# Attention loads in a routed network: even and odd partitions in place of partition blocks

## The chip, the cores and the metric

The kernel runs on one core of one Trainium2 chip. The metric is the device time of one execution in microseconds, the median of several executions; less is better. The kernel uses five engines: TensorE (PE in the rows), VectorE (DVE), ScalarE (ACT), GpSimd (POOL) and SyncE (SP), and 16 DMA engines that move data between the chip's main memory and SBUF, the on-chip memory of 128 partitions. SP issues nearly all the transfers that this text is about.

## The reference, cut to what matters

An attention over windows comes first, then two mixtures of experts on its result. Only the attention is touched by the change.

```
B, H, S, D = 4, 8, 768, 64
for c in range(24):                       # chunks of 32 queries
    k_full = concat([mem_k, k[l_start:r_end]])     # 8 memory rows + up to 56 of context
    v_full = concat([mem_v, v[l_start:r_end]])
    scores = 0.125 * q_c @ k_full.T       # per batch and head
    a = softmax(scores)
    out[c] = a @ v_full
x = out as 3072 tokens x 512
x = moe(x, w_gate, w1, w2)                # 8 experts, capacity 384 tokens each
return moe2(x, ...)                       # top 2 of 8 experts, noisy gate
```

## The kernel before, in words

**Units and tiles.** The attention works on 24 tiles of 128 tokens with all 8 heads. Two tiles make a unit, so there are 12 units. Each unit has three buffers in SBUF, and there are three sets of them (`NB`, line 238): `q` (128 partitions, 4 head pairs, 256 queries), `k` (128 partitions, 2 halves, 4 head pairs, 312 keys) and `v` (128 partitions, 2 halves, 4 head pairs, 8 chunks, 65 columns). Two heads form a pair, and one matmul serves both: 64 of the 128 partitions hold the first head of the pair, the other 64 the second. So that the heads don't mix, `k` and `v` have two halves along the free dimension. Half 0 holds data in the first head's 64 partitions and zeros in the rest; half 1 holds data in the second head's 64 partitions and zeros elsewhere. The zeros are written once, at the start (`clear`, line 259), and every load overwrites only the data.

**Which partitions.** In the kernel before, the first head sits in partitions 32 to 95 and the second in 0 to 31 and 96 to 127 (`lanes`, line 1972, orders the arrays in main memory in the same way). Half 0 of `k` or `v` is therefore one transfer of 64 neighbouring partitions, and half 1 is two transfers of 32 neighbouring partitions each.

**Loading.** `load(u)` (line 285) brings a unit in four groups, in this order: q, all of k, half 0 of v, half 1 of v. `paced` (line 275) sends them: before each group it issues a transfer of one element to a small tile called `behind` (line 278) that reads what the third group before has written, so SP stops there until that group has landed. At most three groups are on their way at a time. Line 280 issues the group's own transfers. All of this is one queue: what SP stops at holds everything behind it.

**Stages.** For each tile there are `scores` (line 296, q times k), `softmax` (line 310: VectorE's maximum and difference, then ScalarE's exponentials, in two instructions since the second head's keys stand in two pieces), `ptrans` (line 329, transposes on TensorE), `av` (line 338, times v), `norm`, `split`, `xtrans` and `logits`. `STAGES` (line 224) fixes the order in which the tiles' stages are issued, written out by hand, and each engine works in that order. After every second tile a further unit is loaded into the buffers that have come free. From tile 18 on, the results are stored to main memory with the same `paced`, behind the last loads. Then the routing of the first mixture of experts starts on VectorE and TensorE, and after it the experts' matrix products, in an order set by a planner with costs of its own (class `Pipe`), which the change does not touch.

Of the kernel before, what the change touches and what calls it, by code (L numbers as in the profile page):

```python
# [8 lines left out]
F32 = mybir.dt.float32  # L9
# [3 lines left out]
AF = mybir.ActivationFunctionType  # L13
# [222 lines left out]
def attention(ctx):  # L236
    nc, tc, t = ctx.nc, ctx.tc, ctx.t
    NB = 3
    KU = 4 * KP + LEFT + RIGHT
    with (  # L240
# [4 lines left out]
        bufs = []  # L245
        for i in range(NB):
            q = ld.tile([128, HP, 256], F32, name=f"q{i}")
            k = ld.tile([128, 2, HP, KU], F32, name=f"k{i}")
            v = ld.tile([128, 2, HP, 8, D + 1], F32, name=f"v{i}")
# [6 lines left out]
        xb = psT.tile([128, 2, 512], F32, name="xb")  # L256
        st = [dict() for _ in range(G)]

        def clear(i, j):
            x = bufs[i][j]  # L260
            if i:
                (nc.vector if i == 1 else nc.gpsimd).memset(x, 0.0)
                return
            for n, (p, h2) in enumerate(((0, 0), (32, 1), (96, 0), (64, 1))):
                (nc.gpsimd if j == 2 or n % 2 else nc.vector).memset(x[p : p + 32, h2], 0.0)

        def warm(n):
            some = ctx.ones16[:, :16].unsqueeze(1).to_broadcast([128, G - 1, 16])
# [6 lines left out]
        def paced(*dmas):  # L275
            if len(flown) >= AHEAD:
                n = len(flown) % 8
                nc.sync.dma_start(behind[:, n : n + 1], flown[-AHEAD])  # L278
            for out, src in dmas:
                nc.sync.dma_start(out, src)  # L280
            while len(out.shape) > 2:
                out = out[:, 0]
            flown.append(out[:1, :1])

        def load(u):
            q, k, v = bufs[u % NB]

            def part(x, src, a, b, h2):
                return x[a:b, h2], src[u, a:b]

            paced((q, t.qT[u]))
            paced(*[part(k, t.kT, *r) for r in ((32, 96, 0), (0, 32, 1), (96, 128, 1))])
            paced(part(v, t.vctx, 32, 96, 0))
            paced(*[part(v, t.vctx, *r) for r in ((0, 32, 1), (96, 128, 1))])

        def scores(i):
            q, k, v = bufs[(i // 2) % NB]
# [12 lines left out]
        def softmax(i):  # L310
            sv = st[i].pop("S").rearrange("p h a k -> p (h a) k")
            if (i * 128) % S == 0:
                nc.vector.memset(sv[:CH, :, :LEFT], NEG)
            if (i * 128 + 128) % S == 0:
                nc.vector.memset(sv[96:, :, KEYS - RIGHT :], NEG)
            mx = wk.tile([128, H], F32, tag="mx", name=f"mx{i}")
            p = wk.tile([128, H, KEYS], F32, tag="p", name=f"p{i}")
            nc.vector.tensor_reduce(mx, sv, axis=AX.X, op=ALU.max)
            nc.vector.tensor_tensor(p, sv, mx.unsqueeze(2).to_broadcast([128, H, KEYS]), op=ALU.subtract)
            pe = wk.tile([128, HP, 2 * KEYS], F32, tag="pe", name=f"pe{i}")  # L320
            ps = p.rearrange("p (h a) k -> p h a k", a=2)
            nc.scalar.activation(pe[:, :, 32:96], ps[:, :, 0], AF.Exp, scale=0.125)
            nc.scalar.activation(
                pe.rearrange("p h (b k) -> p h b k", b=4)[:, :, 0::3], ps[:, :, 1].rearrange("p h (b k) -> p h b k", b=2),
                AF.Exp, scale=0.125,
            )
            st[i]["pe"] = pe

# [141 lines left out]
                counts.pop()()  # L470

        later, counts = [], []
        load(0)
        ctx.early(ld)
        nc.scalar.preload_act_table_set("natural_log_exp_and_others")
        for i in range(NB):
            clear(i, 1)
            clear(i, 2)
            if i:
                load(i)  # L480
        stage = locals()
        for i in range(-2, G - 1):
            if i == 0:
# [8 lines left out]
            u = (i - 1) // 2 + NB  # L492
# [474 lines left out]
def constants():  # L967

    f, g = {}, {}
    f["e8f"] = np.tile(np.arange(E, 0, -1, dtype=np.float32), (128, 1))  # L970
    keep = np.ones((128, E, G), np.float32)
    keep[:, :, 0] = 0.0
    f["keep"] = keep
    f["keys"] = np.tile(np.array([2.0**20] + list(range(E - 1, 0, -1)), np.float32), (128, 1))
    f["cap2"] = np.tile(np.array([C2 - XN] + [C2] * (E - 1), np.float32), (128, 1))
    k0 = (np.arange(1, NT + 1, dtype=np.int64) - (NT + 1) // 2) << 28
    f["cand0"] = np.tile(np.where(k0 >= 0, k0, k0 ^ 0x7FFFFFFF).astype(np.int32).view(np.float32), (128, 1))
    for plan in (FAST, THRIFTY):
        jtab = [np.arange(1, n + 1) << sh for n, sh in zip(plan.nj[1:], plan.shifts[1:])] + [np.zeros(1)]
        f["jtab" + plan.name] = np.tile(np.concatenate(jtab).astype(np.int32), (128, 1))  # L980

    k0 = (np.arange(1, NH + 1, dtype=np.int64) - 64) << 25
    g["candh"] = np.tile(np.where(k0 >= 0, k0, k0 ^ 0x7FFFFFFF).astype(np.int32).view(np.float32), (128, 1))
    g["tri"] = np.triu(np.ones((128, 128), np.float32), 1)
    g["iota"] = np.tile(np.arange(128, dtype=np.float32), (128, 1))

    tok = np.arange(G)[None, :] * 128.0 + np.arange(128)[:, None] - NTOK // 2
    g["tokid"] = tok[:, :, None].astype(np.float32)
    g["slotid"] = (tok + (tok >= 0))[:, :, None].astype(np.float32)
    for low in (32, 128):  # L990
        g[f"cols{low}"] = np.tile(np.arange(128 // low * 3 if low < 128 else NA2, dtype=np.float32) - FAR / low, (128, 1))
    return f, g
# [970 lines left out]
def host_layout(i):  # L1963
    q, k, v, mk, mv = i["q"], i["k"], i["v"], i["mem_k"], i["mem_v"]
    NC = S // CH
    f = {}

    U = B * S // 256
    KU = 4 * KP + LEFT + RIGHT
    qT = q.reshape(B, HP, 2, S // 256, 256, D).transpose(0, 3, 2, 5, 1, 4)  # L1970

    lanes = np.r_[64:96, 0:64, 96:128]
    f["qT"] = qT.reshape(U, 128, HP, 256)[:, lanes]


    kb = np.zeros((B, H, NC // 2 * KP + LEFT + RIGHT, D), np.float32)
    vb = np.ones((B, H, NC // 2 * KP + LEFT + RIGHT, D + 1), np.float32)
    for src, mem, dst in ((k, mk, kb), (v, mv, vb)):
        src = np.pad(src, ((0, 0), (0, 0), (LEFT, RIGHT), (0, 0)))
        for m in range(NC // 2):  # L1980
            dst[:, :, KP * m : KP * m + WIN, :D] = src[:, :, 64 * m : 64 * m + WIN]
            dst[:, :, KP * m + WIN : KP * m + WIN + NMEM, :D] = mem
            dst[:, :, KP * m + WIN + NMEM : KP * m + KP, :D] = src[:, :, 64 * m + WIN : 64 * m + 64]
        dst[:, :, KP * (NC // 2) :, :D] = src[:, :, S:]
    kT = kb.reshape(B, HP, 2, -1, D).transpose(0, 2, 4, 1, 3)
    kT = np.stack([kT[..., 4 * KP * m : 4 * KP * m + KU] for m in range(S // 256)], axis=1)
    f["kT"] = kT.reshape(U, 128, HP, KU)[:, lanes]
    k0 = [KP * (c // 2) + CH * (c % 2) for c in range(NC)]
    vc = np.stack([vb[:, :, o : o + KEYS] for o in k0], axis=3)
    vc = vc.reshape(B, HP, 2, KEYS, S // 256, 8, D + 1).transpose(0, 4, 2, 3, 1, 5, 6)  # L1990
    f["vctx"] = vc.reshape(U, 128, HP, 8, D + 1)[:, lanes]
    f["noise"] = np.ascontiguousarray(i["moe2_noise"].reshape(G, 128, E).transpose(1, 0, 2))
    wg2 = np.concatenate([i["moe2_w_gate"], i["moe2_w_noise"]], axis=1)
    f["wg2"] = np.ascontiguousarray(wg2.reshape(KT, 128, 2 * E).transpose(1, 0, 2))
    for n, m in (("w1", "moe_w1"), ("x1", "moe2_w1")):
        f[n] = np.ascontiguousarray(i[m].reshape(E, KT, 128, 4, FF // 4).transpose(0, 3, 2, 1, 4)).reshape(E, 4, 128, 1024)
    for n, m in (("w2", "moe_w2"), ("x2", "moe2_w2")):
        f[n] = np.ascontiguousarray(i[m].reshape(E, 4, 2, 128, DM).transpose(0, 1, 3, 2, 4)).reshape(E, 4, 128, 1024)
    f["wg"] = np.ascontiguousarray(i["moe_w_gate"].reshape(KT, 128, E).transpose(1, 0, 2))
    f["id32"] = np.eye(128, dtype=np.float32)  # L2000
    for n, c in zip(("consts", "passing"), constants()):
        f[n] = np.concatenate([a.reshape(128, -1).view(np.float32) for a in c.values()], axis=1)
    return f
# [19 lines left out]
```

## Time and profile before

| | |
|---|---|
| median of 3 executions | 1055.89 us (1055.35 to 1056.14) |
| the profiled execution | 1053.0 us, of which the span from first to last instruction is 1051.2 us |
| TensorE busy in the span | 986.2 us (94%) |
| VectorE / ScalarE / GpSimd busy | 642.3 / 461.8 / 296.0 us |
| mean granted TensorE clock | 0.976 |

The span falls in three parts: the attention, up to about 130 us; the first routing, about 131 to 153 us; and the two mixtures of experts, up to the end. How to read the rows further down: times are microseconds from the start of the span; an arrow points from what is read to what is written (`k<-kT_dram` loads k from main memory); L280 is line 280; `SPq` is SP issuing a transfer, and its time is that of the issue, not of the transfer. A "DMA share" of 1.00 means that all 16 DMA engines had a packet in hand throughout.

### The profile page before, as it was taken

How to read it: one execution, taken by the hardware profiler on the slowest of the kernel's cores; microseconds unless marked ns; L12 is line 12 of the kernel's file. 1: busy time of each engine (PE TensorE's matmuls, PEld its weight loads, DVE VectorE, ACT ScalarE, POOL GpSimd, SP SyncE). 2: the span in 40 equal slices, each digit the busy share in tenths (PEclk: the TensorE clock that was granted, in tenths of full speed). 3: DMA queues.
4: the chain of work that ended last, by engine and by line, in shares of the span. 5: the costliest groups of instructions: out<-in, count | busy, mean ns of one | idle time of the engine just before them, and what ended most of it. 6: DMA issues, size and time to landing. Idle time of an engine off the chain costs nothing.

```text
span 1051.2 us, 21987 instructions
## 1 busy us (share of the span) xinstructions
PE 986.2 (94%) x8312; PEld 592.7 (56%) x8312; DVE 642.3 (61%) x2096; ACT 461.8 (44%) x817; POOL 296.0 (28%) x471
## 2 busy tenths in 40 slices
PE   7787649999999999998989999999999999999997
PEld 4676546767676676544555454455555555555553
DVE  6687775666666758695774846545455454564221
ACT  2576514444534446986506535245153351533110
POOL 6565414101102023101021323333233331232321
PEclk9899859999999999999999999999999999999999
DMA  8898833557578486959349748539367393664520
GB/s 238 255 267 235 304 137 123 186 159 210 169 225 203 151 203 192 305 165 201 62 105 268 241 133 244 140 106 260 95 203 176 88 286 87 167 116 110 115 66 31
DMA packets 147253, 184.61 MB, mean 176 GB/s; under 512 B 105558, under 2 KB 106070, under 8 KB 145608
## 3 DMA queue, kind: packets, MB, share of 16 engines
q1 hardware_dynamic: 129814, 131.74, 46.2%
q0 software_dynamic: 13872, 45.15, 14.7%
q10 hardware_dynamic: 3458, 6.30, 1.7%
q8 instruction: 66, 1.08, 0.5%
q14 instruction: 43, 0.35, 0.1%
HBM read 127.10 MB, written 32.44 MB: 152 GB/s over the span
## 4 chain that ended last, share of the span: by engine, by line
PE 71%; DMA 11%; DVE 6%; issue 5%; ACT 3%; SPq 2%; POOL 1%; ACTq 0%; POOLq 0%; DVEq 0%
PE m L68 55%; PE m2f L68 10%; DMA v<-vctx_dram 4%; PE rps L68 3%; DMA k<-kT_dram 1%; DMA yT<-rb 1%; SPq L280 1%; DMA xg<-xr,idx 1%; ACT junk L68 1%; SPq L278 1%; DMA xr<-rb 1%; PE slps L68 1%; PE sb L304 1%; DVE sloh L68 1%; DMA st<-x_dram 1%
## 5 line engine op out<-in xcount | busy, mean ns | idle before, releaser
L68 PEld LDWEIGHTS <-hT 128*128 128x128 f16 (+2 forms) x1800 | 143.5, 99 | 159.5 <-issue 5.1
L68 ACT ACTIVATE hT<-m 128x384 f16<-128x384 f32 (+2 forms) x152 | 75.6, 499 | 274.6 <-PE m L68 271.6
L68 DVE SCALAR_TENSOR_TENSOR hT<-m,hT 128x384 f16<-128x384 f32 (+2 forms) x152 | 86.4, 569 | 96.3 <-ACT hT L68 96.2
L68 ACT ACTIVATE junk<-st 128x1024 f16<-128x1024 f32 x108 | 113.6, 1052 | 61.4 <-DMA st<-x_dram 26.0
L68 PE MATMUL m2f<-st,hT 128*128 128x256 f32 x480 | 127.6, 398 | 0.6 <-ACT hT L68 0.6
L68 POOL DMA_INDIRECT out_dram<-pv,ts x47 | 48.9, 1040 | 257.5 <-DVE pv L68 99.3
L68 DVE SCALAR_TENSOR_TENSOR pv<-m,ys,pv 128x512 f32<-128x512 f32 (+2 forms) x47 | 33.5, 714 | 118.8 <-PE m L68 118.7
L68 PE MATMUL m<-xT,w_0h 128*128 128x384 f16 (+2 forms) x384 | 96.6, 331 | 2.8 <-DMA xT<-xg 2.8
L68 PE MATMUL m<-xT,w_2h 128*128 128x384 f16 (+2 forms) x384 | 96.7, 331 | 1.7 <-DVE hT L68 1.7
L68 PE MATMUL m<-xT,w_1h 128*128 128x384 f16 (+2 forms) x384 | 96.5, 331 | 0.0
L68 PE MATMUL m<-xT,w_3h 128*128 128x384 f16 (+2 forms) x384 | 96.4, 331 | 0.0
L68 PEld LDWEIGHTS m2f<-st,hT 128*128 128x128 f32 x480 | 83.4, 190 | 10.2 <-ACT hT L68 1.0
L68 PE MATMUL m<-w_3h,hT 128*128 128x512 f16 (+2 forms) x300 | 71.6, 345 | 1.4 <-DVE hT L68 1.4
L68 PE MATMUL m<-w_0h,hT 128*128 128x512 f16 (+2 forms) x300 | 72.7, 348 | 0.0
L68 PE MATMUL m<-w_1h,hT 128*128 128x512 f16 (+2 forms) x300 | 72.1, 347 | 0.0
L68 PE MATMUL m<-w_2h,hT 128*128 128x512 f16 (+2 forms) x300 | 71.5, 345 | 0.0
L68 PE MATMUL m<-xT,w_2l 128*128 128x384 f16 (+2 forms) x192 | 63.6, 331 | 0.0
L68 PE MATMUL m<-xT,w_1l 128*128 128x384 f16 (+2 forms) x192 | 63.6, 331 | 0.0
L68 PE MATMUL m<-xT,w_3l 128*128 128x384 f16 (+2 forms) x192 | 63.6, 331 | 0.0
L68 PE MATMUL m<-xT,w_0l 128*128 128x384 f16 (+2 forms) x192 | 63.6, 331 | 0.0
L68 POOL DMA_INDIRECT xg<-x,rows x54 | 53.2, 985 | 29.9 <-issue 11.7
L68 POOL DMA_INDIRECT xg<-xr,idx x24 | 25.0, 1040 | 129.1 <-DVE idx L68 39.0
(336 smaller groups left out, 1870.2 us busy)
## 6 DMA issues: line engine op xcount, KB each, us to landing
st<-w_dram SPq DMA_DIRECT2D x64, 512.0 KB
st<-x_dram SPq DMA_DIRECT2D x64, 512.0 KB
xr<-rb SPq DMA_DIRECT2D x24, 264.0 KB
x<-rb SPq DMA_DIRECT2D x24, 264.0 KB
v<-vctx_dram SPq DMA_DIRECT2D x12, 520.0 KB
v<-vctx_dram SPq DMA_DIRECT2D x24, 260.0 KB
q<-qT_dram SPq DMA_DIRECT2D x12, 512.0 KB
out_dram<-zero ACTq DMA_DIRECT2D x24, 256.0 KB
```

The costliest lines, as they stand in the source:

```text
L68: return f(*args, **kw)
L278: nc.sync.dma_start(behind[:, n : n + 1], flown[-AHEAD])
L280: nc.sync.dma_start(out, src)
L304: nc.tensor.matmul(sc[CH * c : CH * c + CH, hp], q[:, hp, CH * o : CH * o + CH], k[:, :, hp, k0 : k0 + KEYS], start=True, stop=True,)
```

## The change

The first head of a pair takes the even partitions and the second the odd ones (`lanes` becomes 0, 64, 1, 65, ...). Each half of `k` and of `v` is then one transfer of 64 partitions at every second partition. The exponentials of both heads are one instruction, which writes every second column. The buffers are cleared whole, half by half, by VectorE, ScalarE and GpSimd, all of it issued ahead of the first load, and the four small arrays of `ctx.early` are loaded after unit 0's q and k instead of after its v.

```
-        def clear(i, j):
-            x = bufs[i][j]
-            if i:
-                (nc.vector if i == 1 else nc.gpsimd).memset(x, 0.0)
-                return
-            for n, (p, h2) in enumerate(((0, 0), (32, 1), (96, 0), (64, 1))):
-                (nc.gpsimd if j == 2 or n % 2 else nc.vector).memset(x[p : p + 32, h2], 0.0)
+        def clear(i, j, *engines):
+            x = bufs[i][j].rearrange("p a h k -> p a (h k)" if j == 1 else "p a h c d -> p a (h c d)")
+            for h2, e in enumerate(engines):
+                if e is nc.scalar:
+                    e.activation(x[:, h2], zero.to_broadcast([128, x.shape[2]]), AF.Copy)
+                else:
+                    e.memset(x[:, h2], 0.0)
...
-            def part(x, src, a, b, h2):
-                return x[a:b, h2], src[u, a:b]
+            def part(x, src, h2):
+                return x[h2::2, h2], src[u, h2::2]
 
             paced((q, t.qT[u]))
-            paced(*[part(k, t.kT, *r) for r in ((32, 96, 0), (0, 32, 1), (96, 128, 1))])
-            paced(part(v, t.vctx, 32, 96, 0))
-            paced(*[part(v, t.vctx, *r) for r in ((0, 32, 1), (96, 128, 1))])
+            paced(*[part(k, t.kT, h2) for h2 in range(2)])
+            if not u:
+                ctx.early(ld)
+            for h2 in range(2):
+                paced(part(v, t.vctx, h2))
...
-            ps = p.rearrange("p (h a) k -> p h a k", a=2)
-            nc.scalar.activation(pe[:, :, 32:96], ps[:, :, 0], AF.Exp, scale=0.125)
             nc.scalar.activation(
-                pe.rearrange("p h (b k) -> p h b k", b=4)[:, :, 0::3], ps[:, :, 1].rearrange("p h (b k) -> p h b k", b=2),
-                AF.Exp, scale=0.125,
+                pe.rearrange("p h (k a) -> p h a k", a=2), p.rearrange("p (h a) k -> p h a k", a=2), AF.Exp, scale=0.125
             )
...
-        load(0)
-        ctx.early(ld)
+        zero = ld.tile([128, 1], F32, name="zero")
+        nc.vector.memset(zero, 0.0)
         nc.scalar.preload_act_table_set("natural_log_exp_and_others")
+        V_, S_, G_ = nc.vector, nc.scalar, nc.gpsimd
+        for i, (ke, ve) in enumerate((((V_, G_), (S_, V_)), ((G_, G_), (V_, S_)), ((S_, S_), (G_, V_)))):
+            clear(i, 1, *ke)
+            clear(i, 2, *ve)
         for i in range(NB):
-            clear(i, 1)
-            clear(i, 2)
-            if i:
-                load(i)
+            load(i)
...
-    lanes = np.r_[64:96, 0:64, 96:128]
+    lanes = np.arange(128).reshape(2, 64).T.ravel()
```

On SP, at the start of the program, the difference reads as follows (the minus is before, the plus is after; `k_106`, `v_107` and `q_105` are unit 0's buffers, `id`, `c_wg` and `c_noise` the small arrays of `ctx.early`).

```order
 L280 DMA q_105<-qT_dram 128x1024
-L280 DMA k_106<-kT_dram 64x1248
-L280 DMA k_106<-kT_dram 32x1248 x2
+L280 DMA k_106<-kT_dram 64x1248 x2
+L1911 DMA id_138<-id_dram 128x128
+L1888 DMA c_wg<-wg_dram 128x32
+L1888 DMA c_wg_142<-wg_dram 128x64
+L1888 DMA c_noise<-noise_dram 128x192
 L280 DMA v_107<-vctx_dram 64x2080
 L278 DMA behind<-q_105 1x1
-L280 DMA v_107<-vctx_dram 32x2080 x2
+L280 DMA v_107<-vctx_dram 64x2080
```

Two transfers of 32 partitions have become one of 64, in k and in v, and the four small arrays have moved up past both transfers of v.

On SP, in the middle of the loads, where one unit follows another (`k_109`, `v_110` and `q_108` belong to one unit, `q_111` to the next):

```order
 L278 DMA behind<-v_107 1x1
-L280 DMA k_109<-kT_dram 64x1248
-L280 DMA k_109<-kT_dram 32x1248 x2
+L280 DMA k_109<-kT_dram 64x1248 x2
 L278 DMA behind<-v_107 1x1
 L280 DMA v_110<-vctx_dram 64x2080
 L278 DMA behind<-q_108 1x1
-L280 DMA v_110<-vctx_dram 32x2080 x2
+L280 DMA v_110<-vctx_dram 64x2080
 L278 DMA behind<-k_109 1x1
 L280 DMA q_111<-qT_dram 128x1024
```

The order of the groups and of the waits (`behind`) is as before; a unit has five transfers of its own in place of seven.

On ScalarE, at the start (`pe` is the tile of exponentials, `p` the differences, `zero` a single column):

```order
-L475 ACT_TABLE_LOAD
-L322 ACTIVATE pe_208<-p_205 128x4x64
-L323 ACTIVATE pe_208<-p_205 128x4x2x32
+L474 ACT_TABLE_LOAD
+L263 ACTIVATE v_107<-zero 128x2080
+L263 ACTIVATE v_110<-zero 128x2080
+L263 ACTIVATE k_112<-zero 128x1248 x2
+L323 ACTIVATE pe_204<-p_201 128x4x2x64
```

Four clears stand ahead of the first exponential, and two exponentials have become one.

## Rows read from the trace of the kernel before

**Rows 1.** Chain of waits, 56 to 104 us: start, duration, what.

```profile
by line: DMA v<-vctx_dram 58.6%; SPq L280 16.7%; DMA k<-kT_dram 11.7%; SPq L278 9.9%; PE sb L304 4.1%; issue 2.8%; PE xb L346 2.1%; PE pt L333 1.2%; PE xt L400 1.1%; PE Lb L406 0.4%
...
68.07 6.03 DMA v<-vctx_dram
...
74.74 0.57 SPq L280
```

**Rows 2.** Groups of instructions by line up to 130 us: busy, mean ns | idle, releaser.

```profile
L304 PE MATMUL sb<-k,q 128*32 128x128 f32 x768 | 27.4, 287 | 18.8 <-DMA k<-kT_dram 18.8
...
L335 ACT ACTIVATE pts<-pt 128x512 f32<-128x512 f32 x24 | 14.1, 586 | 19.2 <-PE pt L333 19.2
...
L322 ACT ACTIVATE pe<-p 128x256 f32<-128x256 f32 x24 | 10.0, 416 | 17.5 <-DVE p L319 17.0
L323 ACT ACTIVATE pe<-p 128x256 f32<-128x256 f32 x24 | 9.6, 401 | 0.0
```

**Rows 3.** SP's timeline: start, duration of the issues, what, how many.

```profile
1.23 1.74 SPq L280 DMA_DIRECT2D k<-kT_dram  x3
...
21.05 1.65 SPq L280 DMA_DIRECT2D k<-kT_dram  x3
...
69.44 0.91 SPq L280 DMA_DIRECT2D v<-vctx_dram  x2
...
102.89 1.64 SPq L280 DMA_DIRECT2D k<-kT_dram  x3
```

**Rows 4.** Transfers up to 112 us: line's tile, engine, how many, KB each.

```profile
v<-vctx_dram SPq DMA_DIRECT2D x12, 520.0 KB
...
q<-qT_dram SPq DMA_DIRECT2D x12, 512.0 KB
k<-kT_dram SPq DMA_DIRECT2D x12, 312.0 KB
```

**Rows 5.** Stretches: length, busy by engine, clock, DMA share, GB/s.

```profile
2.60:3.40 0.80, 0.80 (x4) 0.37 (x3) 0.80 (x1) 0.00 (x0) 0.80 (x1) 1.00 1.03 415
54.00:55.00 1.00, 1.00 (x32) 0.80 (x24) 0.97 (x5) 0.86 (x3) 0.28 (x1) 1.00 0.92 366
62.80:63.70 0.90, 0.00 (x0) 0.00 (x0) 0.75 (x2) 0.57 (x1) 0.82 (x2) 1.00 0.98 398
56.20:57.20 1.00, 1.00 (x27) 0.96 (x27) 1.00 (x2) 0.41 (x2) 0.99 (x1) 1.00 0.98 229
64.30:65.60 1.30, 1.30 (x36) 1.07 (x31) 0.62 (x2) 0.32 (x3) 0.63 (x3) 1.00 0.92 205
73.00:74.00 1.00, 1.00 (x26) 0.96 (x28) 0.98 (x2) 0.52 (x1) 0.99 (x1) 1.00 0.97 216
```

**Rows 6.** Longer stretches, same columns (PE, PEld, DVE, ACT, POOL).

```profile
38.00:109.00 71.00, 54.54 (x1285) 45.29 (x1280) 55.04 (x189) 45.56 (x93) 42.84 (x103) 0.95 0.89 255
65.00:74.00 9.00, 7.68 (x192) 6.45 (x194) 8.47 (x29) 5.60 (x11) 5.47 (x13) 1.00 0.96 262
...
136.00:148.00 12.00, 5.32 (x107) 4.19 (x108) 8.98 (x48) 0.00 (x0) 0.00 (x0) 0.50 0.02 6
160.00:200.00 40.00, 40.00 (x409) 27.85 (x406) 25.11 (x108) 15.65 (x25) 11.66 (x14) 1.00 0.44 159
```

**Rows 7.** Waits between 100 and 160 us: who waited for whom, us, times, longest.

```profile
POOL xg L68 <- DVE idx L68: 19.7, 1, 19.7
```

**Rows 8.** Timeline of the start: start, duration, engine, what.

```profile
0.76 1.28 ACT L475 ACT_TABLE_LOAD   x1 [0.76 <-PEq L2011]
...
1.07 1.10 DVE L265 MEMSET k<- 32x1248 f32 x1 [1.07 <-PEq L2011]
...
3.69 7.41 POOL L265 MEMSET v<- 32x2080 f32 x4
...
8.75 0.61 SPq L278 DMA_DIRECT2D behind<-k  x1
...
10.91 0.69 DVE L318 TENSOR_REDUCE mx<-sb 128x8 f32<-128x512 f32 x1
```

## The prediction

> **What bounds the kernel now.** I read the chain of waits first, in the attention (56 to 104 us) [rows 1]. The reader is to see that transfers of v and k make up 70% of it, and SP's own issues (lines 280 and 278) another 27%; the computing engines have about a tenth. The groups by line say the same from TensorE's side: the score matmuls stood idle 18.8 us for k [rows 2]. So up to 109 us the kernel goes at the pace at which units land. That pace is read from SP's timeline: unit 2's k is issued at 21.05 and unit 11's at 102.89 [rows 3], nine units in 81.84 us, **9.09 us a unit**.
>
> What comes after passes a shift on unchanged. In 136 to 148 us the DMAs carry nothing (share 0.02) while VectorE and TensorE route [rows 6]; the first gather waits 19.7 us for VectorE's indices [rows 7], not for a store; and from 160 us TensorE is busy 40.00 of 40 us [rows 6]. What the attention gains or loses, the end gains or loses.
>
> Why does a unit take 9.09 us? I took six short stretches and told by the order of issue which transfer fills each [rows 5]. Where q, or half 0 of v (64 neighbouring partitions), moves alone, it goes at 415, and at 366 and 398 GB/s. Where half 1 moves, two transfers of 32 neighbouring partitions, it goes at 229, 205 and 216, with the DMA engines as busy (0.92 to 0.98). So the engines are not short of work; each packet takes nearly twice as long, because of where it goes. I call 382 (the mean of 366 and 398) the fast rate and 217 (the mean of three) the slow one.
>
> A unit's bytes are 512 KB of q, two halves of 312 KB of k and two of 520 KB of v [rows 4], that is 0.524, 0.319 and 0.532 MB. At those rates q takes 1.26 us, half 0 and 1 of k 0.84 and 1.47, of v 1.39 and 2.45: 7.41 us. The remaining 1.68 of 9.09 are gaps: SP stands at a wait, then issues, while less than the full set of engines is fed (share 0.89 over 38 to 109 us [rows 6]).
>
> **The change part by part.**
>
> *The strided transfers.* Bytes, groups and waits are the same; only the partitions differ. No row shows a transfer to every second partition, so both ends: if both halves go at the fast rate, k and v take 1.67 and 2.79 us, with q 5.72 a unit (1.69 less than 7.41). If both go at the slow rate, they take 2.94 and 4.91, with q 9.11 (1.70 more). I take the slow end. [...] This is the choice on which the sign depends.
>
> [...]
>
> *Two issues fewer a unit.* In k, three issues take 1.65 us together [rows 3]; two of 0.57 [rows 1] with a gap of 0.05 take 1.19, or 0.46 less. In half 1 of v, two take 0.91 [rows 3] against 0.57 for one: 0.34. These 0.80 us lie in SP's loop between one landing and the next transfer, and I take them off the gaps: 1.68 becomes 0.88. If slower transfers hide the gaps anyway, the saving is worth nothing and the gaps are between 0 and 0.88; if nothing of it is given, 1.68.
>
> *Sum for a unit:* 9.11 + 0.88 = 9.99, which is 0.90 more than 9.09; over nine units +8.1 us. Bounds on this branch: 9.11 (+0.2 over nine units) and 9.11 + 1.68 = 10.79 (+15.3).
>
> *The start.* Unit 0's k was issued from 1.23 us without waiting [rows 3]. Now half 0 waits for VectorE: a clear of one column, which no row shows, and then the 1.10 us of 1248 columns, from 1.07 on [rows 8], so it is issued near 2.35, and two issues of 0.57 end near 3.5 against 2.97: +0.5. Behind that wait on SP stand all other loads. ScalarE's clear of v stands behind the 1.28 us table load [rows 8]; from 586 ns for 512 columns [rows 2], 2080 take at most 2.4, so it ends by 4.5; SP comes to it after 3.5 with four small arrays to issue first, so I cost that wait at nothing (1.0 if those issues took no time). GpSimd's first half of k is cleared by about 2.5 (its four clears of 2080 columns took 7.41 us [rows 8], 1.85 each, and 1248 columns less). VectorE, at the same 1.85, is through with three such clears near 8.8, where its first maximum stood at 10.91 [rows 8]; this gains nothing, since the third tile's scores wait for unit 1's k at any rate. Between unit 0 and unit 2 two more units pay 0.90 each, and q of unit 1 goes out sooner: the wait ahead of it ended at 8.75 [rows 8], where a semaphore was shared with half 0 of v, and now only k, issued by 3.5, stands there; an estimate from k's and q's bytes at the two rates (1.26 + 2.94 from 3.5) is 7.5, so -1.3. Sum: 0.5 + 1.8 - 1.3 = **+1.0**.
>
> *One exponential for two.* A pair took 416 and 401 ns, overlapping by about 0.1; one of 512 columns took 586 [rows 2]. That is 0.12 less on the path of the tiles behind the last k; three of them, **-0.3**. If writing every second column were as slow as two instructions, 0. Before that, transfers hide it.
>
> *Total:* +8.1 + 1.0 - 0.3 = +8.8 on the profiled execution's 1053.0, or 1061.8. The median of the runs shown is 1055.89, 2.9 above that execution; on its scale 1064.7.
>
> **The rivals.**
>
> *It goes faster: the strided form has the fast rate (0.30).* The mechanism is that a whole half then moves as half 0 of v does now. A unit would need 5.72 + 0.88 = 6.6 us of transfers, and the computing engines take over as the bound: VectorE is busy 55.04 us in 71 [rows 6], 7.8 units, so 7.05 a unit, and it reached at most 8.47 of 9 us, 94% [rows 6]: 7.5 us. I put the pace between 7.5 and 8.0, and nine units give back 9.8 to 14.3. With the start (two more units, and 0.8 us there from the issue) about -2, that is 1040 to 1045, middle 1043. For it: half 1 is the slow part today and goes away in this form. [...] It decides at a rate of 245 GB/s: there k and v (1.704 MB) take 6.95 us, and with q's 1.26 and the gaps' 0.88 the unit is as long as before.
>
> *It goes slower by more (part of the forecast's branch).* The slow rate, and no gap closed: +15.3, and at the start 0.5 + 2 x 1.70 - 1.3 = +2.6, less the 0.3: 1073.5.
>
> *No change (0.10).* The slow rate, but the gaps are filled, because three groups ahead now keep the engines busy throughout: 9.11 a unit, +0.2, with the start's +0.5 (the sooner q is worth nothing then) and the exponentials' -0.3: 1056.3. It is also what a middle rate would give. For it: share 0.89 leaves a tenth to fill. [...]
>
> **How the numbers follow.** The forecast's branch has 0.60: 1058 to 1074, likeliest 1064. Faster has 0.30, no change 0.10. A measurement of this kernel tells a change from about 0.2%, 2.1 us; the branch of no change spreads over both sides of it, so I give it 0.08 for within 0.2%, and 0.01 more to each side. The chances are 0.31, 0.08 and 0.61. The range has to take in the fast branch but for its edge, and the slow one but for its top: 1041 to 1073. The likeliest case's own range is 1058 to 1073.
>
> **What would show it.** In a stretch where one strided half of v moves alone, the rate is near 217 (forecast) or near 380 (rival); at 245 neither is right. Unit 2's to unit 11's k issues lie 90 us apart (forecast), 68 to 72 (rival) or 82 (no change). SP's first issue of k is at 2.3 to 2.5 us. The score matmuls' idle time for k grows from 18.8 to about 27 us, or falls below 8. The exponential takes about 590 ns. From the first routing matmul to the end the distance is as before, within 1 us; if it isn't, the step that passes the attention's shift on unchanged is wrong, and with it every number here.

## The result, and the profile after

The changed kernel takes **1042.39 us** (median of five runs, 1039.98 to 1045.98), the kernel before on the same chip 1056.14 (1055.35 to 1062.72). The ratio is 0.9866, with a 95% interval of 0.9831 to 0.99. The forecast was 1064, slower; what happened is the rival "the strided form has the fast rate", whose middle was 1043, though not at its pace (below). The profiled execution of the changed kernel took 1045.98 us, the slowest of its five runs, with a span of 1044.2.

First the pace. These are rows of SP's timeline of the changed kernel: start and duration of the issues in us, line, what, and how many.

```profile
2.25 1.23 SPq L280 DMA_DIRECT2D k<-kT_dram  x2
6.95 0.49 SPq L280 DMA_DIRECT2D v<-vctx_dram  x1
7.48 0.61 SPq L278 DMA_DIRECT2D behind<-k  x1
8.14 0.37 SPq L280 DMA_DIRECT2D q<-qT_dram  x1
...
18.82 1.17 SPq L280 DMA_DIRECT2D k<-kT_dram  x2
...
92.33 1.62 SPq L280 DMA_DIRECT2D k<-kT_dram  x2
```

Unit 2's k is issued at 18.82 and unit 11's at 92.33, 73.51 us or **8.17 a unit**, against 81.84 and 9.09 before [rows 3]. Nine units give back 8.3 us. Unit 2 is 2.2 us sooner at the start of that stretch, so unit 11 is 10.6 us sooner at its end. Each kernel was profiled once more later (experiments 5 and 6), with paces of 9.31 before and 8.07 changed, so a pace scatters by 0.1 to 0.2 from profile to profile.

Next, the same stretch from unit 2 to unit 11 as one window of each kernel: length, busy time by engine (PE, PEld, DVE, ACT, POOL), granted clock, share of the DMA engines, GB/s. Before:

```profile
21.10:102.90 81.80, 64.94 (x1539) 53.67 (x1539) 62.70 (x212) 51.29 (x108) 45.53 (x108) 0.96 0.87 250
```

After:

```profile
18.80:92.30 73.50, 65.03 (x1499) 52.46 (x1499) 61.69 (x207) 48.32 (x86) 44.45 (x107) 0.97 0.86 286
```

The DMA engines are busy to the same share, 0.87 and 0.86, yet move 250 and 286 GB/s. So it isn't that they are fed better: a busy microsecond carries 16% more (286/0.86 against 250/0.87). That is where the time came from.

The packets in the traces show it directly. Each row of v is one packet of 8320 bytes (1536 of them in each trace, 128 for each of 12 units). In these two windows its median time is 408 ns before and 314 ns after, and 41% of these packets take under 350 ns before, 78% after. So most of the slow packets are gone, but not all: where v's rows move alone, the changed kernel has 297 GB/s in one stretch of its first profile, and 388 in one of its second.

```profile
57.00:58.60 1.60, 0.48 (x19) 0.51 (x23) 1.14 (x5) 1.15 (x3) 1.52 (x5) 1.00 0.93 297
...
31.30:32.30 1.00, 0.32 (x11) 0.20 (x12) 0.88 (x5) 1.00 (x2) 0.79 (x4) 1.00 1.06 388
```

The prediction's first sign, near 217 or near 380 in such a stretch, is therefore not clear-cut here. Why some packets of this form stay slow in the kernel is open.

The groups of instructions by line, changed kernel up to 135 us: busy time and mean ns, then idle time before and what ended it.

```profile
L306 PE MATMUL sb<-k,q 128*32 128x128 f32 x768 | 27.4, 287 | 7.0 <-DMA k<-kT_dram 6.5 <-DVE v L265 0.5
...
L323 ACT ACTIVATE pe<-p 128x512 f32<-128x512 f32 x24 | 16.5, 686 | 8.8 <-DVE p L321 8.1
```

The score matmuls waited 6.5 us for k, where it was 18.8 [rows 2]. The one exponential took 686 ns, where I had taken 586 from another instruction of 512 columns [rows 2].

Last, the hand-over to the routing: the first gather in GpSimd's timeline, of the kernel before and of the changed one.

```profile
152.87 1.18 POOL L68 DMA_INDIRECT xg<-xr,idx  x1 [19.66 <-DVE idx L68]
...
141.87 1.18 POOL L68 DMA_INDIRECT xg<-xr,idx  x1 [19.20 <-DVE idx L68]
```

So the attention hands over 11.0 us sooner. But the span is only 7.0 us shorter: from the first gather to the end are 902.3 us, and 898.3 before. Whether the change did that is the question of experiments 5 and 6.

### The profile page after: what moved, and what is told of

It is laid out like the page before. It is cut to its first block, busy times and chain, and to the rows that moved or that the text cites. A ratio compares the mean times of both kernels' runs of the same rounds, so it can differ in the third digit from the quotient of the medians.

```text
span 1044.2 us, 21927 instructions
## 1 busy us (share of the span) xinstructions
PE 985.8 (94%) x8312; PEld 591.3 (57%) x8312; DVE 641.7 (61%) x2097; ACT 465.2 (45%) x797; POOL 288.6 (28%) x467
## 5 line engine op out<-in xcount | busy, mean ns | idle before, releaser
L68 ACT ACTIVATE hT<-m 128x384 f16<-128x384 f32 (+2 forms) x152 | 75.4, 500 | 280.2 <-PE m L68 262.8
L68 POOL DMA_INDIRECT pv<-out_dram,tg x47 | 46.7, 994 | 49.5 <-DMA out_dram<-pv,ts 33.4
```

The costliest lines, as they stand in the source:

```text
L68: return f(*args, **kw)
```

## The experiments

Each ratio is to runs of the kernel before on the same chip; medians differ between chips (1049 to 1061 for the kernel before), so kernels of different sets are compared by ratio alone. "Pace" is the distance of unit 2's and unit 11's k issues, by nine.

### 1. Blocks of 64 partitions, all else as changed

```diff
-                return x[h2::2, h2], src[u, h2::2]
+                return x[64 * h2 : 64 * h2 + 64, h2], src[u, 64 * h2 : 64 * h2 + 64]
...
-                pe.rearrange("p h (k a) -> p h a k", a=2), p.rearrange("p (h a) k -> p h a k", a=2), AF.Exp, scale=0.125
+                pe.rearrange("p h (a k) -> p h a k", a=2), p.rearrange("p (h a) k -> p h a k", a=2), AF.Exp, scale=0.125
...
-    lanes = np.arange(128).reshape(2, 64).T.ravel()
+    lanes = np.arange(128)
```

> The changed kernel, with the two heads of a pair in partitions 0 to 63 and 64 to 127 instead of the even and the odd ones. Number of transfers, issues, clears, order of loads and the single exponential stay. Theory A (where the rows land decides: 64 neighbours from partition 0 or 64 go at the slow 217 GB/s, every second partition does not): k and v take 2.94 + 4.91 us, with q 9.11, and with 0 to 0.88 of gaps 9.1 to 10.0 a unit, so unit 2's to unit 11's k issues lie 82 to 90 us apart and the time is 1051 to 1059. Theory B (half 1 of before was slow because it was cut into two transfers of 32 rows, wherever they land; a transfer of 64 rows is always fast): like the changed kernel, 73 to 74 us and 1042, or 2 sooner where the exponential with a contiguous write takes 590 instead of 686 ns. Theory C (only the number of issues counts, the rate never mattered): also 73 to 74 us and 1042. [...]

Measured: 1060.2 us against 1049.25, ratio 1.0106 (1.0074 to 1.0137): slower than before. SP's timeline of this kernel:

```profile
21.83 1.16 SPq L280 DMA_DIRECT2D k<-kT_dram  x2
...
111.01 1.81 SPq L280 DMA_DIRECT2D k<-kT_dram  x2
```

Its window between these two:

```profile
21.90:111.00 89.10, 69.02 (x1535) 56.60 (x1524) 62.93 (x211) 49.52 (x89) 45.48 (x108) 0.90 0.99 232
```

Its groups by line:

```profile
L306 PE MATMUL sb<-k,q 128*32 128x128 f32 x768 | 29.8, 304 | 27.5 <-DMA k<-kT_dram 27.5
...
L323 ACT ACTIVATE pe<-p 128x512 f32<-128x512 f32 x24 | 15.1, 629 | 10.2 <-DVE p L321 9.6
```

The pace is 9.91 a unit. The DMA engines are busy all the time (0.99) and move 232 GB/s. The number of transfers, of issues and of rows in each is that of the changed kernel. So theories B (size) and C (issues) fall, and A stands. In the loads, one thing besides the landing place differs: the rows are neighbours in main memory here and every second one in the changed kernel. Experiment 4 reads neighbours in all its forms, and sets that aside. The packets of v's rows have a median of 600 ns in this window, and 4% take under 350.

This kernel is also the one that I forecast under the name of the other: I had 9.99 a unit and about 27 us of idle for k, and this has 9.91 and 27.5.

### 2. The old transfers under the new clears and load order

```diff
-            paced(*[part(k, t.kT, h2) for h2 in range(2)])
+            paced(*[part(k, t.kT, *r) for r in ((32, 96, 0), (0, 32, 1), (96, 128, 1))])
...
-            for h2 in range(2):
-                paced(part(v, t.vctx, h2))
+            paced(part(v, t.vctx, 32, 96, 0))
+            paced(*[part(v, t.vctx, *r) for r in ((0, 32, 1), (96, 128, 1))])
```

(with the two exponentials and the order of lanes of before)

> The changed kernel's clears and early order of loads, with the partitions, the six transfers (32 to 95; 0 to 31 and 96 to 127) and the two exponentials of the kernel before. Theories A, B and C all say that the pace is the old one: unit 2's to unit 11's k issues 81 to 82.5 us apart, and a time of 1053 to 1057 (0 to 2 from the earlier loads at the start). Theory D (the gain comes from the clears and from loads that start sooner, not from the transfers of the units behind): near 1042 to 1046, with the issues still 82 apart.

Measured: 1047.9 us, ratio 0.9978 (0.9954 to 1.0001). SP's timeline:

```profile
20.73 1.64 SPq L280 DMA_DIRECT2D k<-kT_dram  x3
...
104.11 2.64 SPq L280 DMA_DIRECT2D k<-kT_dram  x3
```

The pace is 9.26 (83.4 us for nine units, where 81 to 82.5 were expected), so no faster than the 9.09 and 9.31 of the two profiles of before, and unit 2 is 0.3 us sooner than in [rows 3]. The clears and the order of loads make 0.2% by this ratio, whose interval just reaches no change, and theory D falls.

### 3. As many issues as before, the landing places of the change

```diff
+            def pieces(x, src):
+                return [(x[1::2, 1, a : a + 2], src[u, 1::2, a : a + 2]) for a in (0, 2)]
...
-            paced(*[part(k, t.kT, h2) for h2 in range(2)])
+            paced(part(k, t.kT, 0), *pieces(k, t.kT))
...
-            for h2 in range(2):
-                paced(part(v, t.vctx, h2))
+            paced(part(v, t.vctx, 0))
+            paced(*pieces(v, t.vctx))
```

> The changed kernel, with half 1 of k and half 1 of v each sent as two transfers of two head pairs, to the same every second partitions: as many issues as before the change (three for k, three for v), the rows' landing places unchanged. Theories A and B (the rate made the gain; the issues lie in part beside transfers): the unit grows from 8.17 by at most the 0.80 us of issues, unit 2's to unit 11's k issues 73.5 to 80.7 us apart, and 1042 to 1050; I take half of it, 77 us and 1046. Theory C (the saved issues made the gain, 0.80 of the measured 0.92 us a unit): 81 to 82 us, 1050 to 1053.

Measured: 1037.21 us, ratio 0.9884 (0.9854 to 0.9914), which can't be told from the changed kernel's own ratio. SP's timeline:

```profile
19.69 1.80 SPq L280 DMA_DIRECT2D k<-kT_dram  x3
...
95.11 1.81 SPq L280 DMA_DIRECT2D k<-kT_dram  x3
```

The pace is 8.38, 0.21 and 0.31 more than in the two profiles of the changed kernel (8.17 and 8.07), and the expected 77 us are 75.4. Two issues a unit cost 0.2 to 0.3 us at most, not the 0.80 that I took off, and theory C falls once more.

### 4. The transfers by themselves, in long rows

```diff
...
+    # rows, first partition, step, transfers
+    (128, 0, 1, 6),
+    (64, 32, 1, 12),
+    (64, 0, 1, 12),
+    (64, 0, 2, 12),
...
+            for rows, p0, step, n in PATTERNS:
...
+                sel = slice(p0, p0 + rows * step - step + 1, step)
...
+                    nc.sync.dma_start(big[sel, i * c : i * c + c], t.vctx[u : u + c, :rows].rearrange("c r n -> r c n"))
```

> Leaves out the whole computation and writes zeros: only transfers from HBM to the chip's buffer, of 8320 bytes per row, from SP, eleven patterns one after another (rows, first partition, step): 128 from 0; 64 from 32; 64 from 0; 64 from 0 step 2; 32 from 0; 32 step 2; 32 step 4; 16 from 32 step 4; 16 from 0 step 4; 16 step 8; 16 neighbours. [...] Theory B (size of the transfer): all of 64 rows near 400, those of 32 rows at half. [...]

These windows lie inside the eleven patterns, in the order of that text; the last two columns are the share of the DMA engines and GB/s.

```profile
23.00:31.00 8.00, 0.00 (x0) 0.00 (x0) 1.00 1.00 421
41.00:53.00 12.00, 0.00 (x0) 0.00 (x0) 1.00 0.98 392
61.00:85.00 24.00, 0.00 (x0) 0.00 (x0) 1.00 1.01 206
94.00:106.00 12.00, 0.00 (x0) 0.00 (x0) 1.00 1.00 387
114.00:128.00 14.00, 0.00 (x0) 0.00 (x0) 1.00 1.02 205
137.00:151.00 14.00, 0.00 (x0) 0.00 (x0) 1.00 1.02 206
160.00:168.50 8.50, 0.00 (x0) 0.00 (x0) 1.00 0.98 369
175.00:180.00 5.00, 0.00 (x0) 0.00 (x0) 1.00 0.90 338
185.50:191.50 6.00, 0.00 (x0) 0.00 (x0) 1.00 1.02 204
198.00:205.00 7.00, 0.00 (x0) 0.00 (x0) 1.00 1.02 204
214.00:226.00 12.00, 0.00 (x0) 0.00 (x0) 1.00 1.03 110
```

Read the rows in pairs. 64 neighbours from partition 32 go at 392 GB/s, the same 64 from partition 0 at 206. From 0 with step 2 it is 387 again. 32 rows in step 1 or 2 reach 205 and 206, in step 4 369. Sixteen rows in step 4 reach 338 from partition 32 and 204 from 0 (the eighth window, with a share of 0.90, takes in the end of its pattern). The share is near 1 for fast and slow forms alike, so it tells nothing of this. The time of a packet does: a row of 8320 bytes has a median of 314 ns in each of the five forms at 338 GB/s and more, of 652 to 660 in the five at 204 to 206, and of 1241 in the last.

So the eleven forms fall into three kinds: 338 to 421 GB/s (128 rows, 64 from 32, 64 from 0 in step 2, 32 in step 4, 16 from 32 in step 4), 204 to 206 (64 from 0, 32 in step 1 and in step 2, 16 from 0 in step 4, 16 in step 8) and 110 (sixteen neighbours). Theory B has all of 64 rows near 400 and those of 32 at half: it fails at 64 from 0 (206) and at 32 in step 4 (369). Why a landing place is fast or slow is not shown by these runs.

Against the slow end that the prediction took for every second partition, near 217, stands the fourth row: with step 2, 387.

### 5 and 6. Before and after once more, on one chip

No edit in either.

> The kernel before, once more, for a profile on the chip on which the others of this set run. Unit 2's to unit 11's k issues 81 to 84 us apart (81.84 in the profile shown of before; 83.38 where its transfers ran behind the new clears). From the first gather to the end 893 to 903 us: the profiles so far, which share that part word for word, have 898.3 (before), 902.3 (changed), 894.7, 892.7 and 895.7, so a change of 4 us there would be put down to the run and not to the kernel.

> The changed kernel, once more. Theory A (the attention's gain of 11 us is passed on, and the 4 us that the first profile of it lost behind the first gather came with that run): first gather at 141 to 143, 10 to 12 us sooner than in the kernel before on the same chip, from there to the end 893 to 903, and a ratio to before of 0.985 to 0.991. Theory L (the sooner attention makes the later part longer): from the first gather to the end 901 or more again.

Measured: the kernel before against itself 1050.98 us, ratio 1.0013 (0.9999 to 1.0028); the changed kernel 1036.07 us, ratio 0.9871 (0.9849 to 0.9893). The first gather and the span of the kernel before:

```profile
153.91 1.18 POOL L68 DMA_INDIRECT xg<-xr,idx  x1 [18.06 <-DVE idx L68]
...
core 0: 1050.1 us, clock 0.971
```

and of the changed kernel:

```profile
139.05 1.18 POOL L68 DMA_INDIRECT xg<-xr,idx  x1 [18.06 <-DMA st<-w_dram]
...
core 0: 1032.5 us, clock 0.983
```

Here the attention hands over 14.9 us sooner, more than the 10 to 12 expected, and from the first gather to the end are 896.2 and 893.5 us. The first pair of profiles had 898.3 and 902.3. Over all eleven profiles of the whole kernel these distances run from 892.6 to 902.3 in no order that goes with the edit. So the 4 us lost in the first profile of the changed kernel were that run's, and theory L falls; what makes that part scatter is open. The median gain, 13.1 us here (1049.19 to 1036.07) and 13.75 in the first set, lies between the two shifts of the first gather, 11.0 and 14.9.

### 7 and 8. More transfers under way

Experiment 7 changes one number:

```diff
-AHEAD = 3
+AHEAD = 4
```

> The changed kernel with AHEAD = 4: SP waits for the fourth last group of transfers instead of the third last. Theory G (what is left above the transfers' own 5.72 us of a unit is gaps at SP's waits): the pace falls from 8.17 toward VectorE's 7.5, unit 2's to unit 11's k issues 67 to 70 us apart, the time 3 to 6 us below the changed kernel's. Theory V (VectorE, busy 50.0 of 59 us from 38 to 97, sets the pace already): 72 to 74 us and no difference.

Experiment 8 leaves AHEAD at 3 and puts both halves of v into one group:

```diff
-            for h2 in range(2):
-                paced(part(v, t.vctx, h2))
+            paced(*[part(v, t.vctx, h2) for h2 in range(2)])
```

> The changed kernel with both halves of v in one group: three waits on SP for a unit instead of four, and, three groups ahead, a whole unit under way instead of three quarters. Theory G: as with four groups ahead, and one issue of 0.60 us less a unit, so 66 to 70 us from unit 2's to unit 11's k issues and 3 to 6 us off. Theory V: 72 to 74 us and no difference.

Measured: four ahead 1031.49 us, ratio 0.9838 (0.9815 to 0.9861); one group 1031.49 us, ratio 0.9829 (0.9806 to 0.9852). The changed kernel in the same set had 1036.07. Four ahead, SP's timeline:

```profile
16.00 1.17 SPq L280 DMA_DIRECT2D k<-kT_dram  x2
...
78.77 1.16 SPq L280 DMA_DIRECT2D k<-kT_dram  x2
```

and a window in the middle of its attention:

```profile
38.00:97.00 59.00, 55.10 (x1310) 44.54 (x1304) 54.35 (x185) 43.80 (x77) 41.98 (x98) 1.00 0.92 323
```

The same window of the changed kernel:

```profile
38.00:97.00 59.00, 50.86 (x1196) 41.62 (x1196) 50.03 (x171) 39.76 (x70) 39.15 (x94) 0.97 0.85 283
```

The pace is 6.97 with four ahead and 7.26 with v in one group (issues at 16.13 and 81.43). That is 62.8 us for nine units with four ahead, less than the 67 to 70 expected. VectorE goes from 50.03 to 54.35 us busy in 59. SP's waits for landings (line 278) sum to 23.0 us between 18 and 93 us in the first profile of the changed kernel (9.2 for v, 6.9 each for q and k), and to 7.7 between 16 and 79 with four ahead (4.2, 0.6 and 2.9). So theory G was right for the changed kernel: it still stood at SP's waits, and was not yet bound by VectorE. Both edits are faster than the kernel before and, by 0.4%, than the changed one.

But the loads' pace is no longer the kernel's. These are VectorE's maxima of tile 4 and tile 22, the first tiles of units 2 and 11, with four ahead and, below, in experiment 6:

```profile
25.23 0.68 DVE L320 TENSOR_REDUCE mx<-sb 128x8 f32<-128x512 f32 x1
...
93.17 0.68 DVE L320 TENSOR_REDUCE mx<-sb 128x8 f32<-128x512 f32 x1
```

```profile
26.27 0.68 DVE L320 TENSOR_REDUCE mx<-sb 128x8 f32<-128x512 f32 x1
...
97.79 0.68 DVE L320 TENSOR_REDUCE mx<-sb 128x8 f32<-128x512 f32 x1
```

The tiles go at 7.55 a unit with four ahead (and with v in one group), against 7.95 in experiment 6, where the loads' pace was 8.07. Unit 11's k is issued 12.6 us sooner than in experiment 6 (91.35), and the first gather comes only 4.6 us sooner (134.45), which is what the time gains.

### 9. The kernel before with four ahead

```diff
-AHEAD = 3
+AHEAD = 4
```

> The kernel before with AHEAD = 4 and nothing else. Theory G for the old transfers (its 9.09 us a unit are 7.41 at the rates read and 1.68 of gaps, and a fourth group under way closes most of the gaps): 7.6 to 8.2 a unit, unit 2's to unit 11's k issues 68 to 74 us apart, and 1036 to 1042 where the kernel before takes 1049; then the rate is worth only what the deeper queue leaves, about 0.7 a unit against the 6.97 us a unit of the changed kernel with four ahead. Theory R (the slow landing of half 1 bounds the unit, whatever is queued): 80 us or more, 1046 to 1050.

Measured: 1053.74 us against 1060.84, ratio 0.9935 (0.9907 to 0.9964). SP's timeline:

```profile
19.51 1.64 SPq L280 DMA_DIRECT2D k<-kT_dram  x3
...
96.92 2.25 SPq L280 DMA_DIRECT2D k<-kT_dram  x3
```

and its window:

```profile
38.00:97.00 59.00, 50.35 (x1163) 41.26 (x1159) 48.03 (x162) 39.62 (x82) 37.05 (x93) 0.95 0.97 270
```

Neither theory has it: the pace is 8.60, between the 8.2 of one and the 8.9 (80 us) of the other. The share is 0.97, so its gaps are closed, and still it moves only 270 GB/s. With four ahead on both sides, the old landing places cost 8.60 - 6.97 = 1.63 a unit. The rates that I had read from the trace of before gave 7.41 - 5.72 = 1.69. That they agree so well is luck: both paces lie about 1.2 above the sums by these rates, in experiment 9 with the DMA engines busy (0.97), while in experiment 7 the loads only run ahead of the computing. The tiles go at 8.71 a unit here and at 7.55 in experiment 7, 1.16 apart.

### 10. Both edits

```diff
-AHEAD = 3
+AHEAD = 4
...
-            for h2 in range(2):
-                paced(part(v, t.vctx, h2))
+            paced(*[part(v, t.vctx, h2) for h2 in range(2)])
```

> The changed kernel with both halves of v in one group and AHEAD = 4. Theory V (at 6.97 us a unit, with VectorE busy 54.35 of 59 us, the computing sets the pace): 61 to 65 us from unit 2's to unit 11's k issues and a time within 2 us of the two kernels that have one of the edits. Theory G (SP's waits still cost): the pace falls toward 6.2 to 6.6, 56 to 60 us, and 3 us or more off.

Measured: 1039.01 us against 1060.84, ratio 0.9808 (0.9767 to 0.9849), which overlaps the intervals of 7 and 8. The pace is 7.07 (14.36 to 78.00). SP's waits, from 18 to 85 us, as who waited for whom, us, times, longest:

```profile
SPq L280 <- PE xb L344: 10.8, 6, 3.3
SPq L280 <- PE Lb L442: 6.0, 3, 3.2
SPq L280 <- DMA v<-vctx_dram: 2.2, 2, 1.3
```

Now the loads wait for TensorE to free the buffers (10.8 and 6.0 us), and hardly for landings. That is theory V: the computing sets the pace (the tiles go at 7.70 a unit, 7.55 in experiments 7 and 8), and no gain from further depth is shown. Which of the computing engines it is, these runs don't separate.

### 11. The transfers one at a time

The edit to experiment 4, besides its list of forms: SP waits for each transfer before it issues the next. The question is whether one transfer alone shows the same difference between the forms as a row of them.

```diff
-                for i in range(n - 3, n):
                     nc.sync.dma_start(behind[:, nb : nb + 1], big[p0 : p0 + 1, i * c, :1])
```

> Leaves out the whole computation and writes zeros. Transfers of 8320 bytes per row (532 KB each) from SP, one at a time: SP waits for each before it issues the next, six of each form: 64 rows from 32; 64 from 0 step 2; 64 from 0; 64 from 1 step 2; 32 from 0 step 4 (two rows' worth each); 32 from 0. [...]

SP's timeline, for one pair of rows of the first three forms each: 64 from 32, 64 from 0 step 2, 64 from 0. The time is from the start of the issue to the start of the row under it, which waits for the landing.

```profile
28.59 0.54 SPq L38 DMA_DIRECT2D big<-vctx_dram  x1
32.77 0.59 SPq L39 DMA_DIRECT2D behind<-big  x1
...
51.79 0.52 SPq L38 DMA_DIRECT2D big<-vctx_dram  x1
55.34 0.57 SPq L39 DMA_DIRECT2D behind<-big  x1
...
77.55 0.51 SPq L38 DMA_DIRECT2D big<-vctx_dram  x1
82.27 0.57 SPq L39 DMA_DIRECT2D behind<-big  x1
```

That is 4.18, 3.55 and 4.72 us; over the six of each form it is 3.7 to 4.2, 3.4 to 3.6 and 4.6 to 4.8. Alone, too, the form of step 2 is far from 64 from 0, by 1.2 us in the mean of six, and even half a microsecond quicker than 64 from 32; why it is, is open.

## Why the prediction was wrong

**The step that failed** is "I take the slow end", for the strided transfers. That choice was my estimate, and no run had shown it: I took the fast rate of 64 neighbours to come from their lying side by side. Experiment 4 shows that it does not: 64 neighbours have 392 GB/s from partition 32 and 206 from 0, and every second partition has 387. Half 0 of before had one of the forms with the full rate in experiment 4 (64 from 32, at 392) and half 1 a form with half of it (32 from 0, at 205; its other part, 32 from 96, was not tried alone); the strided form has the full rate (from partition 1, as half 1 has it, a transfer alone lands in 3.4 to 3.6 us in experiment 11, as from 0). The 9.11 us in the forecast's sum stand on that choice. No run shows 64 rows at every second partition near 217 GB/s: in its place experiment 4 has 387, and the two stretches of the changed kernel above have 297 and 388.

**The forecast fits the kernel with slow halves.** With both halves truly slow (experiment 1) the unit takes 9.91, forecast 9.99, and the ratio is 1.0106, where 1061.8 on 1053.0 is 1.0084. So the kernel forecast was experiment 1. That the pace agrees so closely is luck, though: the sum was 9.11 of transfers and 0.88 of gaps, and with a share of 0.99 experiment 1 has about 0.1 of gaps and 9.8 of transfers. The split was wrong for the kernel before, too: its share of 0.89 [rows 6] leaves 0.11 x 9.09 = 1.0 us a unit without a packet, not 1.68.

**The rates read from six short stretches were near.** 382 and 217 were read [rows 5], and the transfers alone have 387 to 392 and 205 to 206. In experiments 9 and 7 the difference per unit is 1.63, where these gave 1.69, which is luck, as told there.

**The saved issues were mis-sized.** I took 0.80 us a unit off the gaps; experiment 3 gives 0.2 to 0.3 at most. My reading is that with three groups under way most of an issue lies beside transfers. So the changed kernel came to 8.17 and not into the rival's 7.5 to 8.0: at 387 for k and v and 421 for q (128 partitions) a unit is 1.704 MB / 387 + 0.524 / 421 = 4.40 + 1.25 = 5.65, which leaves 2.52, not 0.88. Less than half of that is gaps: the share of 0.86 leaves 0.14 x 8.17 = 1.1 us a unit without a packet. In the other 1.4 the DMA engines are busy, a little of it with other transfers (the window moves 21.0 MB, nine units 20.1), the rest with packets that take longer than in experiment 4 (for v's rows a mean of 407 ns, where the median is 314). Experiment 7 takes 1.2 off the loads' pace with one more group under way, so about half of the 2.52 hangs on SP's waits. The rival's floor of 7.5, from VectorE's busy time, fits what the tiles then reach, 7.55.

**The start** went as told in its first steps. SP's first k is issued at 2.25 (2.3 to 2.5 forecast), and its two issues took 1.23 (1.19 forecast). The wait ahead of unit 1's q ended at 7.48 (7.5 forecast, 8.75 before [rows 8]), but that is luck: 3.5 + 1.26 + 2.94 is 7.7, not 7.5, the 2.94 was the slow rate, and in the trace SP stands at no wait for k there. It is still issuing until 7.44, when the second half of v has gone out (6.95 + 0.49). The sum of 1.0 later turned into 2.2 sooner, since the 0.90 that I charged to each of two units has the other sign (from unit 0's k to unit 2's it is 16.57 us, where it was 19.82). The rest of the start is small: with the old transfers unit 2's k is issued at 20.73 (experiment 2), against 21.05 and 20.27 in the two profiles of before, where my +0.5 and -1.3 make 0.8 sooner.

**The exponential** takes 686 ns, not 590. In experiment 1 the same instruction, with a contiguous write, takes 629. So the write to every second column costs 57 ns, and the other 43 come from taking another instruction of 512 columns as its price. Against 416 and 401 ns that overlapped by 0.1 it gains about 0.03 a tile, so -0.3 is -0.1.

**Passing on** the attention's shift holds, but not "within 1 us": the distance from the first gather to the end (the prediction had named the first routing matmul) scatters by up to 10 us between profiles. One profile of each kernel can't test it (11.0 sooner and only 7.0 passed on in the first pair, 14.9 and 17.6 in the second); the medians' 13.1 and 13.75 agree with it within that scatter.

## What to carry to other kernels

Two transfers that keep the DMA engines equally busy can differ by two in rate (387 and 206 GB/s at shares of 1.00 and 1.01, experiment 4): look at GB/s beside the share, and ask of the slow one where its rows land. Here every second partition out of 128 (387 GB/s) is as good a landing place as 64 neighbours from 32 (392), and 64 neighbours from 0 are half as good (206). Where a sign hangs on such a rate that no row shows, it is better to hold both ends near even than to choose by an argument on how the engines work inside. After the rate is mended, see whether the queue is deep enough to use it: here one more group under way gave about another 0.4% (1036.07 to 1031.49 us, experiment 7), and then the computing set the pace.

## What the runs showed that was not expected

A share near 1 of the DMA engines goes with anything from 110 to 421 GB/s (experiment 4). One transfer of 520 KB alone lands 3.5 to 4.7 us after its issue (experiment 11), though at 387 GB/s its bytes take 1.4; the difference between step 2 and 64 from 0 is still the 1.2 us of the two rates (2.58 - 1.38), but that is only a quarter of 4.7. An exponential of 128 x 512 that writes every second column takes 686 ns against 629 for contiguous columns. And a part of the program that is word for word the same in all kernels, from the first gather to the end, takes 892.6 to 902.3 us from profile to profile.
